# Attention beside a Fourier layer on one core: triangle selections one block after their softmax without a mark, and a store queued behind the next block's transposition

## Chip, cores and metric

One core of a Trainium2 chip runs the whole program. The metric is the device time of one execution in microseconds (us). Before the change it is 1834.63 us, the median of three runs (1828.07 to 1836.04).

## What is computed

Two independent layers on inputs of 2048 rows by 1024 columns, their outputs set side by side (2048 x 2048, fp32):

```
qkv    = (A_x @ A_wqkv), cut into 32 heads of width 32
scores = q @ k.T * 32**-0.5, kept where 0 <= i - j < 256, else -1e9
a      = concat_heads(softmax(scores) @ v) @ A_wo
b      = dft_seq_re @ (B_x @ dft_hid_re.T) - dft_seq_im @ (B_x @ dft_hid_im.T)
out    = concatenate([a, b], axis=-1)
```

The factors of the first layer are drawn eight times larger, so the softmax is sharp and the kernel works in pairs of fp16 numbers: every fp32 operand is split into a high and a low half (hi and lo), and a product is made of three matmuls (hi x hi, hi x lo, lo x hi).

## The kernel before

**The long products.** TensorE does almost nothing but matmuls of 128 x 128 weights against 512 columns, called products here. First come the projections of q, k and v (`product`, L341, matmuls on L347), then the Fourier layer: units of kind "x" (the hidden transform, again `product`) and units of kind "c" (the sequence transform, `seven`, L813, matmuls on L825, tiles p_a, p_b, p_c), and last the output projection (tiles po_a to po_c, also L825). Their operands are split by ScalarE (ACT) and VectorE (DVE), and ACT and DVE empty their accumulators (tiles y, L817 and L819).

**Attention in small blocks among them.** `attention` (L175) is a generator. Every eight product matmuls (four in `seven`) call `tick`, which lets it take its next step when it is due. There are 256 blocks: 8 groups of 4 heads, 4 chunks of 512 rows, 2 halves of the heads (2 heads each), 4 rows of 128 queries. Step b, with halves j = 0 and 1, does this:

- `s_step` (L197): the scores of one head by matmul (L214) into tile s, two buffers in PSUM. After the second head (j = 1) the softmax of the block: DVE masks the corner by a predicated copy (L222) and takes the maximum mx (L224); ACT makes the bias (L227), the exponentials (L234, one per head) and the high half hi (L237); DVE makes the low half lo (L238). Both go to tile hl, and SyncE (SP) issues a DMA that transposes hl into t (L240). Tile t has the packed weights of at most two key blocks: where a row of queries sees three, the first and the last are both triangles and share one square.
- `z_step` (L243): parts that packed square on GpSimd (POOL). A first selection writes one triangle to tile z (L252, four buffers), a second clears it from t in place (L254).
- `v_step` (L258): weights times values for a pair of blocks (e, e+1), e even, by matmul (L282) into tile pv (one PSUM bank, which the transposes of `scale_of` use too); the pair's second block comes first, and it needs that block's z and t. DVE divides by the row sums (L288 to L293) into tile o. It is issued LAG = 6 steps after the pair's first block.
- `o_step` (L298): every eight blocks, ACT and DVE split o into ohl; SP transposes it by DMA into ot (L305) and stores ot to DRAM as ots (L306). o, ohl and ot share three buffers. ots is read only in the output projection at the end (`o_load`, L782, its DMAs on L786).

**What sets the order.** The code is recorded in the order above. A list scheduler then gives each engine its own fixed order: of the instructions that its timeline holds ready, the one recorded first. Each engine runs its order strictly and waits on semaphores where an operand or a buffer is not ready. So an instruction that is recorded early but is ready late in that timeline goes behind later ones, and one wait holds everything behind it on that engine. SP's order holds all loads, transpositions and plain stores; POOL's holds the selections, small fills, and the adding stores of the Fourier layer's results (L909). `tc.issue_after(x)` fixes an instruction behind x on x's engine.

**The mark.** After the bias of every odd block, POOL copies one column of it to tile mark (L231). Before the change the first selection of a block is fixed behind the latest mark, and so are the adding stores. `z_step` is called in pairs: at odd b, after block b's softmax is recorded, for blocks b-3 and b-2.

Of the kernel before, what the change touches and what calls it, by code (L numbers as in the profile page):

```python
# [16 lines left out]
ALU = mybir.AluOpType  # L17
AX = mybir.AxisListType

P = 128  # L20
# [30 lines left out]
def fused_kernel(ctx: ExitStack, tc: tile.TileContext, xa, wqk, wv, wo, xb, wd, cs, out):  # L51
    nc = tc.nc
# [4 lines left out]
    ots = tc.dram_tile((NCH, P, NG, 2, CH), F16, name="ots")  # L57
# [24 lines left out]
                            fill=0.0, base=0, pattern=[[1, P]], channel_multiplier=-1)  # L82
# [43 lines left out]
    marks = []  # L126
# [48 lines left out]
    def attention():  # L175
# [2 lines left out]
                  for hp in range(2) for i in range(QB)]  # L178
        nblk = len(blocks)
        st, cur, q2s, k2s, vts = {}, {}, {}, {}, {}  # L180

        def do_load(g, sc):
            if (g, sc) in q2s:
                return
            for d, kind, parts, bufs in ((k2s, 1, (0, 0, 1), 3), (q2s, 0, (0, 1, 0), 2)):
                u = att.tile([96, HG, CH], F16, tag=f"qk{kind}", bufs=bufs, name=f"qk{kind}_{g}_{sc}")
                for j, part in enumerate(parts):
                    nc.sync.dma_start(u[32 * j:32 * j + 32],
                                      qs[kind, g, sc, part].rearrange("(h d) t -> d h t", d=DH))
                d[g, sc] = u  # L190

            vt = att.tile([P, QB, HG * VW], F16, tag="vt", bufs=3, name=f"vt_{g}_{sc}")
            nc.sync.dma_start(vt, vs[sc * QB:sc * QB + QB, :, g * HG * VW:(g + 1) * HG * VW]
                              .rearrange("t p c -> p t c"))
            vts[g, sc] = vt

        def s_step(b, j):  # L197
            g, sc, hp, i = blocks[b]
            qb = sc * QB + i
            nb = min(qb + 1, 3)  # L200
            if j == 0:
                if i == 0:
                    do_load(g, sc)
                st[b] = {"s": ps_s.tile([P, 2, 512], F32, tag="s", name=f"s_{b}")}
            if j == 1 and hp == 1 and i == 0 and b + QB < nblk and (g, sc + 1) in ready:
                do_load(*blocks[b + QB][:2])
            d = st[b]
            h = 2 * hp + j
            s = d["s"]
            k0 = qb + 1 - nb  # L210
            while k0 <= qb:
                k1 = min(qb + 1, (k0 // QB + 1) * QB)
                at = (k0 - (qb - 2)) * P
                nc.tensor.matmul(s[:, j, at:at + (k1 - k0) * P], q2s[g, sc][:, h, i * P:i * P + P],  # L214
                                 k2s[g, k0 // QB][:, h, k0 % QB * P:k0 % QB * P + (k1 - k0) * P],
                                 start=True, stop=True, skip_group_check=True)
                k0 = k1
            if j == 0:
                return
            w = min(nb, 2) * P  # L220
            sv = s[:, :, 3 * P - w:3 * P]
            nc.vector.copy_predicated(s[:, :, 2 * P:3 * P], upper2, s[:, :, :P] if nb == 3 else never2)  # L222
            mx = att.tile([P, 2], F32, tag="mn", bufs=6, name=f"mx_{b}")
            nc.vector.tensor_reduce(mx, sv, axis=AX.X, op=ALU.max, negate=True)  # L224
            bias = att.tile([P, 2], F32, tag="bias", bufs=6, name=f"bias_{b}")
            es = esc[g][:, sc:sc + 1]
            nc.scalar.activation(bias, mx, AF.Identity, bias=pshift, scale=es)  # L227
            if b % 2 == 1:

                mark = att.tile([P, 1], F32, tag="mark", bufs=2, name=f"mark_{b}")  # L230
                marks[:] = [nc.gpsimd.tensor_scalar(mark, bias[:, 0:1], 1.0, None, op0=ALU.mult)]  # L231

            for h in range(2):
                nc.scalar.activation(sv[:, h], sv[:, h], AF.Exp, bias=bias[:, h:h + 1], scale=es)  # L234
            hl = att.tile([P, 8 * P], F16, tag="hl", bufs=3, name=f"hl_{b}")
            hi, lo = (hl[:, a * w:a * w + 2 * w].rearrange("p (h k) -> p h k", h=2) for a in (0, 2))
            nc.scalar.activation(hi, sv, AF.Copy)  # L237
            behind[:] = [nc.vector.tensor_tensor(lo, sv, hi, op=ALU.subtract)]  # L238
            t = att.tile([P, 8, P], F16, tag="t", bufs=6, name=f"t_{b}")
            nc.sync.dma_start_transpose(t[:, :4 * min(nb, 2)], hl[:, :4 * w])  # L240
            d["t"] = t

        def z_step(b):  # L243

            g, sc, hp, i = blocks[b]
            if sc * QB + i < 2:
                return
            d = st[b]
            pk = d["t"].rearrange("p (a k) q -> p a k q", k=2)[:, :, 1]
            z = att.tile([P, 4, P], F16, tag="z", bufs=4, name=f"z_{b}")  # L250
            with tc.issue_after(marks[0].ins):
                nc.gpsimd.affine_select(out=z, in_=pk, compare_op=ALU.is_gt, fill=0.0, base=0,  # L252
                                        pattern=[[0, 4], [-1, P]], channel_multiplier=1)
            nc.gpsimd.affine_select(out=pk, in_=pk, compare_op=ALU.is_ge, fill=0.0, base=0,  # L254
                                    pattern=[[0, 4], [1, P]], channel_multiplier=-1)
            d["z"] = z
# [41 lines left out]
        def o_step(g, sc):  # L298

            o = cur.pop((g, sc)).rearrange("p i c -> p (i c)")  # L300
            ohl = att.tile([P, 2, CH], F16, tag="o", bufs=3, name=f"ohl_{g}_{sc}")
            nc.scalar.activation(ohl[:, 0], o, AF.Copy)
            nc.vector.tensor_tensor(ohl[:, 1], o, ohl[:, 0], op=ALU.subtract)
            ot = att.tile([P, 2 * QB, P], F16, tag="o", bufs=3, name=f"ot_{g}_{sc}")
            nc.sync.dma_start_transpose(ot, ohl.rearrange("p h c -> p (h c)"))  # L305
            nc.sync.dma_start(ots[sc, :, g].rearrange("c h t -> c (h t)"), ot.rearrange("p a q -> p (a q)"))  # L306

        for b in range(nblk + LAG):
            for j in range(2):
                yield blocks[b][:2] if b < nblk else None  # L310
                if b < nblk:
                    s_step(b, j)
                if j == 1 and b % 2 == 1 and 3 <= b < nblk + 3:
                    z_step(b - 3)
                    z_step(b - 2)
                if j == 0 and b % 2 == 0 and b >= LAG:
                    v_step(b - LAG)
                    g, sc, hp, i = blocks[b - LAG + 1]
                    if hp == 1 and i == QB - 1:
                        o_step(g, sc)  # L320

    acc = [0.0]
    agen, upcoming = [None], [None]
# [385 lines left out]
    with tc.tile_pool(name="pa", bufs=2) as pa:  # L709
        for n, (kd, g, c) in enumerate(order):  # L710
# [4 lines left out]
            if n == START:  # L715
                agen[0] = attention()
                upcoming[0] = next(agen[0])
# [3 lines left out]
            if kd == "v":  # L721
                t = c
# [127 lines left out]
    with tc.tile_pool(name="pb", bufs=1) as pb:  # L850
# [56 lines left out]
        def store(dst, src):  # L907
            with tc.issue_after(marks[0].ins):
                nc.gpsimd.dma_start(dst, src, accum_op=ALU.add)  # L909
# [6 lines left out]
        for n, (kind, p, c, i) in enumerate(units):  # L916
            if kind == "x":
# [13 lines left out]
                else:  # L931
                    a = pair.pop()
# [92 lines left out]
```

## Time and profile before

| what | us |
|---|---|
| median of three runs | 1834.63 |
| lowest and highest run | 1828.07, 1836.04 |
| span of the profiled execution, first to last instruction | 1822.3 |
| TensorE busy in it | 1756.3 |
| VectorE, ScalarE, GpSimd busy | 1325.8, 1093.0, 406.9 |

No run time is listed for the profiled execution by itself; its span is 12.3 us below the median of the runs, which is what lies around the span together with the difference between runs. TensorE busy time counts each matmul with its latency, so a busy TensorE may still lose time; idle time is certain loss. In the profile PE is TensorE, PEld its weight loads, and "idle before" is what an instruction's engine waited just ahead of it.

### The profile page before, as it was taken

The numbers are of one execution on the slowest core, as the hardware profiler recorded it, in microseconds if no ns is written. First come the engines' busy times: TensorE is split into PE (matmuls) and PEld (weight loads), VectorE is DVE, ScalarE is ACT, GpSimd is POOL, SyncE is SP. The second block draws the span as 40 slices with busy tenths as digits, with TensorE's granted clock in tenths as the row PEclk, the third lists the DMA queues.
The fourth block names the chain that finished last, engine by engine and source line by source line (L and its number), as shares of the span: only waits on it lengthen the run. The fifth ranks groups of instructions, "written<-read, shape, count | busy, mean of one in ns | idle before, by whom it ended". The sixth has DMA issues, their size and how long they took to land.

```text
span 1822.3 us, 30052 instructions
## 1 busy us (share of the span) xinstructions
PE 1756.3 (96%) x10876; PEld 857.3 (47%) x10876; DVE 1325.8 (73%) x2362; ACT 1093.0 (60%) x1867; POOL 406.9 (22%) x666
## 2 busy tenths in 40 slices
PE   7999999999999999999989899998989999999998
PEld 3444545555545544555444444544544554444443
DVE  7665887778766788886788686888876788577442
ACT  3333554556556777776777676777776678463322
POOL 0000222222212222322123233323333223200000
PEclk9999999999999999999999999999999999999999
DMA  5357898978767656899548989756998746855331
GB/s 231 115 176 209 211 249 216 237 176 215 183 144 166 128 123 156 183 197 214 111 100 173 197 182 199 162 127 128 188 176 191 151 93 128 226 109 98 110 93 70
DMA packets 440598, 297.96 MB, mean 164 GB/s; under 512 B 339072, under 2 KB 396416, under 8 KB 440448
## 3 DMA queue, kind: packets, MB, share of 16 engines
q1 hardware_dynamic: 433536, 270.87, 62.1%
q0 software_dynamic: 6912, 25.17, 8.4%
q8 instruction: 85, 1.39, 0.3%
q14 instruction: 65, 0.53, 0.1%
HBM read 146.93 MB, written 75.63 MB: 122 GB/s over the span
## 4 chain that ended last, share of the span: by engine, by line
PE 73%; DVE 9%; issue 7%; DMA 6%; ACT 4%; POOL 2%; SPq 0%; POOLq 0%; DVEq 0%; ACTq 0%
PE p L347 13%; PE p_a L825 10%; PE pv L347 9%; PE pk L347 9%; PE pq L347 8%; PE p_b L825 5%; PE po_a L825 5%; DMA t<-hl 3%; PE s L214 3%; PE pv L282 3%; PE p_c L825 3%; PE po_b L825 2%; PE po_c L825 1%; DVE raw_u L626 1%; DMA out_dram<-reg 1%
## 5 line engine op out<-in xcount | busy, mean ns | idle before, releaser
L347 PE MATMUL p<-reg,un 128*128 128x512 f16 x1536 | 345.1, 379 | 0.0
L234 ACT ACTIVATE s<-s,bias,escs 128x256 f32<-128x256 f32 (+1 forms) x512 | 267.4, 528 | 10.6
L227 ACT ACTIVATE bias<-mx,pshift,escs 128x2 f32<-128x2 f32 x256 | 97.5, 383 | 242.7 <-DVE mx L224 210.8
L231 POOL TENSOR_SCALAR mark<-bias 128x1 f32<-128x1 f32 x128 | 42.8, 334 | 846.0 <-ACT bias L227 831.5
L347 PEld LDWEIGHTS <-un 128*128 128x128 f16 x1536 | 146.5, 98 | 164.9
L238 DVE TENSOR_TENSOR hl<-s,hl 128x512 f16<-128x512 f32 (+1 forms) x256 | 169.7, 666 | 74.5 <-ACT hl L237 72.5
L825 PE MATMUL p_a<-reg,un_c 128*128 128x512 f16 x768 | 186.0, 384 | 6.4 <-ACT p_c L832 4.9
L347 PE MATMUL pq<-reg,wu_q 128*128 128x512 f16 x768 | 177.8, 386 | 6.9 <-ACT reg L113 4.3
L254 POOL TENSOR_SCALAR_AFFINE_SELECT t<-t 128x512 f16<-128x512 f16 x224 | 181.2, 881 | 0.1
L347 PE MATMUL pk<-reg,wu_k 128*128 128x512 f16 x768 | 175.1, 379 | 0.9 <-ACT wu_k L113 0.5
L347 PE MATMUL pv<-reg,reg 128*128 128x512 f16 x768 | 174.0, 379 | 0.0
L224 DVE TENSOR_REDUCE mx<-s 128x2 f32<-128x512 f32 (+1 forms) x256 | 169.5, 666 | 2.4
L252 POOL TENSOR_SCALAR_AFFINE_SELECT z<-t 128x512 f16<-128x512 f16 x224 | 155.4, 712 | 48.9 <-DMA t<-hl 48.3
L237 ACT ACTIVATE hl<-s 128x512 f16<-128x512 f32 (+1 forms) x256 | 148.3, 583 | 9.8 <-DMA t<-hl 5.0
L222 DVE COPY_PREDICATED s<-upper,s 128x256 f32<-128x256 uint32 x224 | 94.0, 422 | 60.1 <-PE s L214 55.5
L214 PE MATMUL s<-qk,qk 96*128 96x128 f16 (+2 forms) x704 | 128.7, 276 | 3.4 <-DVE hl L238 3.4
L282 PE MATMUL pv<-vt,t 128*128 128x65 f16 x1984 | 114.3, 186 | 11.6 <-POOL t L254 11.2
L347 PEld LDWEIGHTS <-wu_q 128*128 128x128 f16 x768 | 75.3, 99 | 96.0 <-issue 13.2
L825 PEld LDWEIGHTS <-un_a 128*128 128x128 f16 x768 | 74.8, 99 | 93.1 <-issue 8.5
L825 PEld LDWEIGHTS <-un_c 128*128 128x128 f16 x768 | 74.4, 99 | 92.6 <-issue 10.2
L825 PEld LDWEIGHTS <-un_b 128*128 128x128 f16 x768 | 73.4, 98 | 89.2 <-issue 5.3
L282 PEld LDWEIGHTS <-t 128*128 128x128 f16 x1984 | 97.8, 97 | 35.1 <-POOL t L254 14.9
(175 smaller groups left out, 2873.1 us busy)
## 6 DMA issues: line engine op xcount, KB each, us to landing
raw_u<-in_cs_dram SPq DMA_DIRECT2D x64, 512.0 KB, 4.8
qk<-qs SPq DMA_DIRECT2D x192, 128.0 KB, 3.2
out_dram<-y POOLq DMA_DIRECT2D x36, 512.0 KB, 7.5
raw_u<-in_xb_dram SPq DMA_DIRECT2D x32, 512.0 KB, 5.2
vs<-yv SPq DMA_DIRECT2D x32, 260.0 KB, 2.8
vt<-vs SPq DMA_DIRECT2D x32, 260.0 KB, 4.3
raw_x<-in_xa_dram SPq DMA_DIRECT2D x16, 512.0 KB, 10.2
qs<-yq SPq DMA_DIRECT2D x32, 256.0 KB, 2.2
```

Of the source, the lines that this page charges most:

```text
L214: nc.tensor.matmul(s[:, j, at:at + (k1 - k0) * P], q2s[g, sc][:, h, i * P:i * P + P], k2s[g, k0 // QB][:, h, k0 % QB * P:k0 % QB * P + (k1 ...
L222: nc.vector.copy_predicated(s[:, :, 2 * P:3 * P], upper2, s[:, :, :P] if nb == 3 else never2)
L224: nc.vector.tensor_reduce(mx, sv, axis=AX.X, op=ALU.max, negate=True)
L227: nc.scalar.activation(bias, mx, AF.Identity, bias=pshift, scale=es)
L234: nc.scalar.activation(sv[:, h], sv[:, h], AF.Exp, bias=bias[:, h:h + 1], scale=es)
L237: nc.scalar.activation(hi, sv, AF.Copy)
L238: behind[:] = [nc.vector.tensor_tensor(lo, sv, hi, op=ALU.subtract)]
L252: nc.gpsimd.affine_select(out=z, in_=pk, compare_op=ALU.is_gt, fill=0.0, base=0, pattern=[[0, 4], [-1, P]], channel_multiplier=1)
L254: nc.gpsimd.affine_select(out=pk, in_=pk, compare_op=ALU.is_ge, fill=0.0, base=0, pattern=[[0, 4], [1, P]], channel_multiplier=-1)
L282: nc.tensor.matmul(pvt[:, r, j, lo:], weights(part, j, kb), vts[g, k // QB][:, k % QB, at + lo:at + VW], start=(m == 0), stop=(m == len(se ...
L347: nc.tensor.matmul(ps, lhs(hl, d), rhs(hr, d), start=(m == 0), stop=(m == 3 * n - 1))
L825: nc.tensor.matmul(ps, lhs[pos](hl, k), rhs(pos)[:, hr, k], start=(m == 0 and pos < 2), stop=(m == 11), skip_group_check=True)
```

## The change

Three edits. The selections of a block are called one step after its softmax, block by block (`z_step(b - 1)` at every step), in place of two blocks at a time, two and three steps after. Their tie to the mark goes; the marks stay, for the adding stores. The store of ot is kept back in a list and recorded after the transposition of the next block whose softmax is recorded, fixed behind it on SP; after the last blocks it is issued at once.

```diff
+        held_back = []
...
-            nc.sync.dma_start_transpose(t[:, :4 * min(nb, 2)], hl[:, :4 * w])
+            moved = nc.sync.dma_start_transpose(t[:, :4 * min(nb, 2)], hl[:, :4 * w])
             d["t"] = t
+            for store in held_back:
+                with tc.issue_after(moved.ins):
+                    store()
+            held_back.clear()
...
-            with tc.issue_after(marks[0].ins):
-                nc.gpsimd.affine_select(out=z, in_=pk, compare_op=ALU.is_gt, fill=0.0, base=0,
-                                        pattern=[[0, 4], [-1, P]], channel_multiplier=1)
+            nc.gpsimd.affine_select(out=z, in_=pk, compare_op=ALU.is_gt, fill=0.0, base=0,
+                                    pattern=[[0, 4], [-1, P]], channel_multiplier=1)
...
-            nc.sync.dma_start(ots[sc, :, g].rearrange("c h t -> c (h t)"), ot.rearrange("p a q -> p (a q)"))
+            held_back.append(lambda: nc.sync.dma_start(ots[sc, :, g].rearrange("c h t -> c (h t)"),
+                                                       ot.rearrange("p a q -> p (a q)")))
...
-                if j == 1 and b % 2 == 1 and 3 <= b < nblk + 3:
-                    z_step(b - 3)
-                    z_step(b - 2)
+                if j == 1 and 1 <= b < nblk + 1:
+                    z_step(b - 1)
...
                         o_step(g, sc)
+                        if b >= nblk:
+                            held_back.pop()()
```

## The prediction

> **What bounds the kernel.** I read the page's busy shares first, then busy time by stretches, cut where TensorE's busy tenths change, then who waited for whom.
>
> ```profile
> PE 1756.3 (96%) x10876; PEld 857.3 (47%) x10876; DVE 1325.8 (73%) x2362; ACT 1093.0 (60%) x1867; POOL 406.9 (22%) x666
> ```
> ```profile
> 98.00:950.00 852.00, 848.04 (x5556) 423.72 (x5554) 644.75 (x1206) 526.15 (x935) 195.75 (x356) 1.00 0.75 178
> 950.00:1556.00 606.00, 568.99 (x3772) 281.92 (x3771) 472.88 (x877) 432.80 (x764) 199.61 (x286) 0.98 0.80 161
> ```
>
> The second block's columns are the stretch, its length, then busy time of PE, PEld, DVE, ACT and POOL, the granted clock, the DMA share and GB/s. TensorE is the bound. From 98 to 950 us it idles 4 us of 852, so nothing that helps attention can gain there. From 950 to 1556 it idles 37 us of 606, at a mean clock of 0.98: that is where the change can act for the better. After 1556 there is almost no attention left.
>
> What TensorE waits for in that stretch, and what lies behind it:
>
> ```profile
> PE pv L282 <- POOL t L254: 11.2, 11, 2.2
> PE pv L282 <- POOL z L252: 10.1, 3, 6.1
> POOL z L252 <- DMA t<-hl: 41.9, 21, 6.6
> SPq L306 <- DMA ot<-ohl: 16.7, 9, 4.3
> ```
>
> The figures are total us, times, longest. Waits of the value matmuls on the selections (21.3 us here) are the largest part of the 37. POOL in its turn waits 21 times for a transposition that has not landed. SP waits nine times with the store of ot for its transposition, and what stands behind it waits too. The worst case shows the links (SP first, then POOL, then PE):
>
> ```profile
> 948.65 1.24 SPq L305 DMA_TRANSPOSE ot<-ohl  x1
> 954.28 0.33 SPq L306 DMA_DIRECT2D ots<-ot  x1
> 954.71 2.69 SPq L240 DMA_TRANSPOSE t<-hl  x2
> ```
> ```profile
> 954.55 0.21 POOL L231 TENSOR_SCALAR mark<-bias 128x1 f32<-128x1 f32 x1 [8.03 <-ACT bias L227]
> 954.71 0.64 POOL L252 TENSOR_SCALAR_AFFINE_SELECT z<-t 128x512 f16<-128x512 f16 x1
> 958.14 0.71 POOL L252 TENSOR_SCALAR_AFFINE_SELECT z<-t 128x512 f16<-128x512 f16 x1 [2.80 <-DMA t<-hl]
> ```
> ```profile
> 958.90 0.23 PE L282 MATMUL pv<-vt,z 128*128 128x65 f16 x1 [6.05 <-POOL z L252]
> ```
>
> The transpositions stood behind the store, which stood behind ot's landing; both mark and landing were late, and the landing came last. So a mark alone is not what TensorE waits for here.
>
> **Clock.** Stretches cut at the clock's steps:
>
> ```profile
> 956.53:963.35 6.82, 3.96 (x31) 1.87 (x32) 4.57 (x8) 2.88 (x6) 2.34 (x3) 0.50 0.51 116
> 1031.50:1033.70 2.20, 0.24 (x3) 0.01 (x1) 2.20 (x3) 0.71 (x2) 2.14 (x2) 1.00 0.88 165
> 1035.03:1038.45 3.42, 3.42 (x10) 1.23 (x9) 1.89 (x5) 1.65 (x4) 0.21 (x1) 0.50 1.12 208
> 1272.00:1274.40 2.40, 0.17 (x3) 0.05 (x1) 2.40 (x4) 2.40 (x5) 2.35 (x2) 1.00 0.87 207
> 1362.71:1369.54 6.83, 6.35 (x36) 3.00 (x37) 2.85 (x7) 2.11 (x5) 2.24 (x5) 0.50 0.83 237
> 1550.45:1553.86 3.41, 3.41 (x29) 1.76 (x30) 2.32 (x5) 0.00 (x0) 3.34 (x4) 0.50 0.97 183
> ```
>
> Four stretches at half clock, 20.5 us together, follow or hold such waits: about 10.2 us of lost product time, 0.48 us for each of the 21.3 us waited.
>
> **The change part by part.** No instruction is added or removed but order; 448 selections and 32 stores move.
>
> *Mark and early calls.* A pair's selections, which stood behind the bias of a block two later, may now start when their packing lands. On paper that removes at most the 21.3 us and the 10.2 us of clock: 31.5 us. One buffer rule takes part of the advance: with four buffers z, the selection of an even block e must wait for the value matmuls of pair e-4. Those stand ahead of the scores of e+1 in the new order, or within 1 us of them, well before e's packing can land, so I price this wait at nothing; without that cover it would hold marks, fills and adding stores behind it on POOL. These stores also come behind selections that wait for a landing; they write tiles y, of which there are four, and POOL is busy only 199.6 of 606 us, so nothing again, at worst some us.
>
> *Store kept back.* SP no longer stands still for the 16.7 us; at most the nine cases with it gain. ots is read at the very end, and the buffer of ot is wanted a chunk (eight blocks) later, which hides the delay; if it did not, DVE's write of o would wait.
>
> *What the scheduler makes of it.* This is the term that decides. I counted in the fixed order of both kernels how many 512-column products stand on TensorE between the last score matmul of a pair's second block and the pair's first value matmul. That count is the time that softmax, transposition and selection have before TensorE stops. For the first 49 pairs (to about 670 us) the orders of TensorE are the same: 96.9 products on the mean. For the other 79 pairs it falls from 80.7 to 55.2; for the last 30 from 79.5 to 49.7, mostly exactly 48. The value matmuls stay where they were among the products; the scores stand later. A product costs 0.216 us:
>
> ```profile
> 109.06 20.72 PE pk L347 x96
> ```
>
> So 5.5 us of slack is gone on the mean, 6.4 us at the end, and 17.4 us of products become 11.9 (10.7 at the end). Scores and an earlier value group in between add about 1.7 us at most (estimate: the timeline's 0.49 us for two score matmuls, twice, and some 0.7 us for narrow matmuls), so 13.6 us on the mean, 12.4 at the end.
>
> Against it, the chain from scores to selected triangles, by rows:
>
> ```profile
> L234 ACT ACTIVATE s<-s,bias,escs 128x256 f32<-128x256 f32 x214 | 111.0, 528 | 3.4
> L254 POOL TENSOR_SCALAR_AFFINE_SELECT t<-t 128x512 f16<-128x512 f16 x98 | 91.5, 1069 | 0.1
> L238 DVE TENSOR_TENSOR hl<-s,hl 128x512 f16<-128x512 f32 x109 | 72.4, 668 | 38.2 <-ACT hl L237 38.0
> L224 DVE TENSOR_REDUCE mx<-s 128x2 f32<-128x512 f32 x107 | 70.5, 665 | 0.5
> L252 POOL TENSOR_SCALAR_AFFINE_SELECT z<-t 128x512 f16<-128x512 f16 x98 | 70.4, 732 | 41.9 <-DMA t<-hl 41.9
> L237 ACT ACTIVATE hl<-s 128x512 f16<-128x512 f32 x109 | 63.1, 584 | 6.4 <-DMA t<-hl 5.0
> L227 ACT ACTIVATE bias<-mx,pshift,escs 128x2 f32<-128x2 f32 x107 | 40.4, 382 | 69.2 <-DVE mx L224 66.3 <-DVE sc_u L107 1.3 <-DVE rs L288 1.1
> L222 DVE COPY_PREDICATED s<-upper,s 128x256 f32<-128x256 uint32 x95 | 39.5, 421 | 21.8 <-PE s L214 20.2 <-PE pv L282 1.0
> ```
> ```profile
> DMA to landing us min/median/max: 2.4/3.8/15.0
> ```
>
> Bare, with nothing in the way: 0.42 + 0.67 + 0.38 + 2 x 0.53 + 0.58 + 0.67 = 3.8 us to the low half, 3.8 us median landing, 0.73 + 1.07 us of selection: 9.4 us. That fits. But DVE is busy 78% and ACT 71% of this stretch, and the landing reaches 15 us. A pair as it ran (PE scores, SP, POOL, PE values):
>
> ```profile
> 1271.62 0.49 PE L214 MATMUL s<-qk,qk 96*128 96x384 f16 x2
> 1294.59 0.19 PE L282 MATMUL pv<-vt,z 128*128 128x65 f16 x1
> ```
> ```profile
> 1277.89 5.64 SPq L240 DMA_TRANSPOSE t<-hl  x2
> ```
> ```profile
> 1291.17 0.94 POOL L252 TENSOR_SCALAR_AFFINE_SELECT z<-t 128x512 f16<-128x512 f16 x1 [0.25 <-DMA t<-hl]
> ```
>
> Its values came 22.5 us after its scores, with 84 products between (block 206). The new order leaves 50 there: 34 x 0.216 = 7.3 us less, 15.2 us. Its packing landed 19 us after the scores. TensorE would have stood about 5 us.
>
> *The sum.* In the stretch POOL waited for landings in 21 cases; 98 selections z are 49 pairs. Such a landing comes after the mark of a block one pair later. A pair passes every 606 / 49 = 12.4 us and its mark needs 0.42 + 0.67 + 0.38 us, so it is at least 13.9 us after the scores, plus a mean wait of 2.0, plus 1.8 of selection: 17.7 us, against 12.9 us (between the two means above): 4.8 us late, 21 times: 101 us. But the next pair's scores mostly stand just ahead of the waiting value matmul, so one pair's wait is slack for the next one: I take half, 50 us (bounds: nothing, if every chain is bare; 101, if none is relieved). At 0.48 us of clock each, 24 us more. Off go 21.3, 10.2, and half of SP's 16.7. Before 950 us the slack is larger, about 15 us; I add 2 us. Sum: 50 + 24 - 21.3 - 10.2 - 8.3 + 2 = +36 us on a span of 1822.3. Added to the median, 1834.63 + 36 = **1871 us**.
>
> *A rule weighed.* The clock term rests on the 1031.50 row (2.2 us almost idle, half clock soon after) against the 1272.00 row (2.4 us, no such stretch shown). The Trainium skill, TensorE: Matmul & The Clock Gate, Part 1, has the clock halve after an idle window of about 3.4 us that runs freely; the stretches of 3.41 and 6.83 us agree with that window, the 1031.50 row shows that less idling can do. By that page alone waits of 2 to 3 us would mostly cost no clock; that is rival 2.
>
> **Rivals.**
>
> 1. *Faster: the chain is close to bare.* Place: the landing of the second block's packing. If it comes within about 11 us of the scores (13 less 1.8), the value matmuls never wait, and the whole 21.3 + 10.2 us goes: 1803 us; with some waits left, up to 1825. For it: 9.4 us bare, SP free of its 16.7, scores later and so less crowded by earlier work. Against: 21 landings of 49 are beyond 13.9 us. Chance 0.20.
> 2. *Waits without clock.* As forecast, but short waits cost no half clock: 36 - 24 = +12, 1847 us. Chance 0.10.
> 3. *No relief.* The chain's own DVE and ACT steps stand behind work that waits for the same stopped TensorE, so each wait comes in full: 101 + 48 - 21.3 - 10.2 - 8.3 + 2 = +111, 1946 us. For it: in the new order the low half of block 207 stands on DVE behind a product's add that needs TensorE 6.5 us on; 6.5 + 0.67 + 3.8 + 1.8 = 12.8, already over 12.3. Chance 0.07.
> 4. *Like for like.* Old waits go, as many come: 1835 us. The change then does not do what it says in effect, though it moves all it names. Chance 0.08.
>
> **How the numbers follow.** Forecast, chance 0.55: 1871, itself 1847 to 1908 (new waits of 34 to 75 us for the 50, each with its clock). To hold 8 in 10, the range leaves out rival 3 (0.07) and the faster half of rival 1 (0.10): 1812 to 1925. A measurement here tells about 0.5% from no change, 9 us. Faster by more: rival 1, 0.20. Within: rival 4 and a fifth of rival 2, 0.10. Slower by more: the rest, 0.70.
>
> **What the new profile would show.** Right: TensorE's waits on z and t after 680 us come to 40 to 60 us in some 20 to 40 cases, spread over pairs and not only beside ot's stores; POOL's idle time before z is put down to the landing, more than 41.9 us; half-clock stretches in greater number; SP's wait with the store near nothing; 98 to 650 us unchanged. Wrong: few such waits, landings within 11 us of the scores (rival 1); or new waits of the products themselves on DVE or ACT, which the reordering may bring and for which I have no row.

## The result, and the profile after

| | before | after |
|---|---|---|
| median (lowest to highest), us | 1832.38 (1828.07 to 1836.04) | 1899.41 (1897.04 to 1906.29) |
| ratio to before, 95% interval | | 1.038 (1.035 to 1.0411) |
| profiled execution: time, span, us | span 1822.3 | 1906.29, 1904.6 |

The change makes the kernel 3.8% slower: 67 us between the medians, 82.3 us between the two profiled spans. In the execution after only 1.7 us lies around the span, so the "12.3 us" of the text above was nearly all difference between runs: with 1.7 us around its span, the profiled execution of before took some 1824 us, under the lowest time listed, while that of after is the longest of its four. What follows accounts for the 82.3 us.

The busy shares of the page, then its stretches with the same columns as before:

```profile
PE 1783.0 (94%) x10876; PEld 862.9 (45%) x10876; DVE 1329.4 (70%) x2362; ACT 1093.5 (57%) x1867; POOL 435.5 (23%) x666
```
```profile
98.00:650.00 552.00, 551.30 (x3567) 274.98 (x3566) 402.11 (x753) 301.01 (x536) 128.64 (x239) 1.00 0.79 191
650.00:950.00 300.00, 291.61 (x1937) 145.17 (x1934) 242.99 (x443) 220.50 (x391) 86.31 (x114) 1.00 0.66 154
950.00:1556.00 606.00, 525.58 (x3331) 254.90 (x3330) 409.60 (x766) 378.79 (x669) 178.88 (x248) 0.94 0.72 146
```

The kernel before had, in the first two of these stretches:

```profile
98.00:650.00 552.00, 551.12 (x3567) 274.98 (x3565) 401.19 (x753) 300.80 (x536) 118.11 (x237) 1.00 0.78 191
650.00:950.00 300.00, 296.92 (x1991) 148.74 (x1989) 243.56 (x454) 225.35 (x400) 77.64 (x119) 1.00 0.69 155
```

The same instructions run. From 98 to 650 us TensorE does not differ. By 950 us it is 54 matmuls behind. From 950 to 1556 it idles 80 us where it idled 37, at a mean clock of 0.94 where it was 0.98, and gets through 441 matmuls fewer (3331 against 3772); all these run after 1556 us. Over the whole span, idle time of TensorE rises from 66.0 to 121.6 us (+55.6), and its busy time by 26.7 us with the same matmuls: the slower clock.

What TensorE waits for, by the waits (total us, times, longest):

```profile
PE pv L286 <- POOL z L256: 48.6, 20, 6.7
PE pv L286 <- POOL t L258: 13.2, 21, 1.5
PE p_a L831 <- DVE y L825: 7.7, 9, 2.1
PE p_a L831 <- ACT y L823: 7.7, 3, 4.4
PE s L215 <- DVE hl L239: 6.6, 3, 3.4
```

Waits of the value matmuls on the two selections are 61.8 us; over the whole trace of before they were 22.3 (+39.5):

```profile
PE pv L282 <- POOL t L254: 11.2, 11, 2.2
PE pv L282 <- POOL z L252: 11.1, 4, 6.1
```

The long products' waits on ACT and DVE (p_a, p_b, p_c, all rows) went from 15.9 to 28.0 us (+12.1), the scores' wait for their buffer from 3.4 to 6.6.

One pair shows how; it is the pair of block 206, which the prediction followed before. Scores of block 207, and its softmax, selection and values, from the timeline (start, length, engine, line, what it is, idle before):

```profile
1330.80 0.49 PE L215 MATMUL s<-qk,qk 96*128 96x384 f16 x2
...
1337.85 2.75 PE L831 MATMUL p_a<-reg,un_b 128*128 128x512 f16 x12
1340.56 2.75 PE L831 MATMUL p_a<-reg,un_a 128*128 128x512 f16 x12
1343.15 0.82 PE L215 MATMUL s<-qk,qk 96*128 96x128 f16 x6
1346.70 0.20 PE L286 MATMUL pv<-vt,z 128*128 128x65 f16 x1 [2.73 <-POOL z L256]
1346.74 0.20 PE L286 MATMUL pv<-vt,t 128*128 128x65 f16 x1
1348.28 0.20 PE L286 MATMUL pv<-vt,t 128*128 128x65 f16 x1 [1.35 <-POOL t L258]
```
```profile
1333.49 0.38 ACT L228 ACTIVATE bias<-mx,pshift,escs 128x2 f32<-128x2 f32 x1
1333.77 1.14 ACT L113 ACTIVATE un_a<-raw_u,sc_u 128x1024 f16<-128x1024 f32 x1
1334.81 0.71 ACT L113 ACTIVATE reg<-raw_u,sc_u 128x512 f16<-128x512 f32 x1
1335.42 1.05 ACT L619 ACTIVATE junk<-raw_u 128x1024 uint8<-128x1024 f32 x1
1336.37 0.19 ACT L619 ACTIVATION_READ_ACCUMULATOR junk<-raw_u 128x1 f32 x1
1336.46 1.09 ACT L235 ACTIVATE s<-s,bias,escs 128x256 f32<-128x256 f32 x2
```
```profile
1340.43 0.68 DVE L239 TENSOR_TENSOR hl<-s,hl 128x512 f16<-128x512 f32 x1
```
```profile
1341.13 3.65 SPq L241 DMA_TRANSPOSE t<-hl  x2
```
```profile
1346.00 0.64 POOL L256 TENSOR_SCALAR_AFFINE_SELECT z<-t 128x512 f16<-128x512 f16 x1 [8.29 <-DMA t<-hl]
```

Counted from the end of the scores, as in the prediction, the values come after 15.4 us; before it was 22.5. The packing lands after 14.7 us; before it was 19. So the chain did get shorter, but less than the room did, and TensorE stands 2.73 + 1.35 us. Of the chain, 2.6 us pass between the bias and the exponentials, in which ACT works on another operand (L113, L619); 2.2 more between the end of the high half (0.60 us on ACT, from 1337.58) and the low half on DVE; and 4.9 us from the issue to the landing. Waits like this come about every 26 us from 1300 to 1510 us.

### The profile page after: what moved, and what is told of

Same layout as the page of the kernel before. It is cut to its first block, busy times and chain, and to the rows that moved or that the text cites. A ratio compares the mean times of both kernels' runs of the same rounds, so it can differ in the third digit from the quotient of the medians.

```text
span 1904.6 us, 30082 instructions
## 1 busy us (share of the span) xinstructions
PE 1783.0 (94%) x10876; PEld 862.9 (45%) x10876; DVE 1329.4 (70%) x2362; ACT 1093.5 (57%) x1867; POOL 435.5 (23%) x666
## 4 chain that ended last, share of the span: by engine, by line
PE 67%; DMA 11%; DVE 10%; ACT 5%; issue 3%; POOL 3%; SPq 0%; POOLq 0%; DVEq 0%; ACTq 0%
PE p L353 10%; PE p_a L831 9%; PE pv L353 9%; PE pk L353 9%; PE pq L353 8%; DMA t<-hl 8%; PE p_b L831 5%; PE po_a L831 4%; PE pv L286 3%; PE p_c L831 3%; PE s L215 3%; PE po_b L831 2%; DMA out_dram<-y 2%; POOL z L256 1%; DMA out_dram<-reg 1%
## 5 line engine op out<-in xcount | busy, mean ns | idle before, releaser
L256 POOL TENSOR_SCALAR_AFFINE_SELECT z<-t 128x512 f16<-128x512 f16 x224 | 171.4, 765 | 878.9 <-DMA t<-hl 774.5
L353 PE MATMUL p<-reg,un 128*128 128x512 f16 x1536 | 349.9, 381 | 1.4 <-ACT reg L930 1.4
L286 PE MATMUL pv<-vt,z 128*128 128x65 f16 (+1 forms) x896 | 98.3, 188 | 48.9 <-POOL z L256 48.6
L831 PEld LDWEIGHTS <-un_a 128*128 128x128 f16 x768 | 77.4, 102 | 101.5 <-issue 21.3
L831 PEld LDWEIGHTS <-un_b 128*128 128x128 f16 x768 | 73.6, 98 | 95.1 <-issue 12.3
## 6 DMA issues: line engine op xcount, KB each, us to landing
raw_x<-in_xa_dram SPq DMA_DIRECT2D x16, 512.0 KB, 10.2
```

Of the source, the lines that this page charges most:

```text
L286: nc.tensor.matmul(pvt[:, r, j, lo:], weights(part, j, kb), vts[g, k // QB][:, k % QB, at + lo:at + VW], start=(m == 0), stop=(m == len(se ...
L353: nc.tensor.matmul(ps, lhs(hl, d), rhs(hr, d), start=(m == 0), stop=(m == 3 * n - 1))
L831: nc.tensor.matmul(ps, lhs[pos](hl, k), rhs(pos)[:, hr, k], start=(m == 0 and pos < 2), stop=(m == 11), skip_group_check=True)
```

## The experiments

Each kernel ran beside the kernel before on the same chip; that had a median of 1830.39 us beside the first four, 1831.94 beside the next four, 1825.46 beside the last three. So the ratios are to be compared, not the medians. "Products" is the count on which the prediction rests: 512-column products on TensorE between the last score matmul of a pair's second block and its first value matmul, mean of the 79 pairs from block 98 on. "Selections" is TensorE's wait on z and t, "half clock" the time at a granted clock of 0.5 from 98 us to the last matmul, both from the profiled execution.

| kernel | products | selections, us | half clock, us | median, us | ratio (interval) |
|---|---|---|---|---|---|
| before | 80.7 | 22.3 | 27.3 | | 1 |
| after | 55.2 | 61.8 | 78.5 | 1899.41 | 1.038 (1.035 to 1.0411) |
| held store alone | 80.7 | 23.6 | 27.3 | 1825.07 | 0.9977 (0.9954 to 1.0) |
| mark's tie out, early calls | 61.1 | 60.6 | 78.5 | 1893.87 | 1.0345 (1.0297 to 1.0393) |
| after, five buffers z | 55.2 | 59.2 | 85.3 | 1901.49 | 1.0394 (1.0336 to 1.0453) |
| after, products behind scores (2) | 78.1 | 31.2 | 51.2 | 1837.27 | 1.0037 (1.001 to 1.0064) |
| early calls, mark kept | 59.1 | 43.8 | 61.4 | 1874.61 | 1.0229 (1.0198 to 1.026) |
| after, products behind scores (4) | 65.3 | 53.3 | 64.9 | 1881.4 | 1.0292 (1.0238 to 1.0346) |
| after, products behind scores (1) | 88.1 | 19.7 | 51.2 | 1823.98 | 0.9961 (0.9935 to 0.9987) |
| held store, behind scores (1) | 87.3 | 31.3 | 54.6 | 1824.94 | 0.9968 (0.9942 to 0.9995) |
| held store, (1) from block 151 | 83.5 | 31.7 | 41.0 | 1821.37 | 0.9969 (0.9948 to 0.9991) |
| after, (1) from block 151 | 76.6 | 17.5 | 41.0 | 1825.76 | 1.0003 (0.9978 to 1.0028) |
| held store, (1) blocks 151 to 196 | 81.4 | 24.1 | 34.1 | 1819.82 | 0.997 (0.9946 to 0.9995) |

The theory was the prediction's: the change takes products, that is time, from between a pair's scores and its values. Rivals: the selections off the mark wait for their own buffers; the missing tie to the mark itself; the store.

**The store alone.** The held-back store of the change on the kernel before, nothing else. The orders of TensorE, DVE, ACT and POOL are those of before; only SP's differs.

> Only the held-back store; selections and mark as before. The fixed orders of TensorE, VectorE, ScalarE and GpSimd are those of before, and only 83 places of SP's order differ. Theory 1 (the scores stand too close ahead of the value matmuls, 55 products in place of 81, so the chain from scores to selections does not fit): here 81 products stand, so no loss; SP's 16.7 us of waits with the store go, and part of TensorE's 21 us of waits on selections with them: 0 to 12 us faster than before, 1820 to 1833 us. Rival 3 (the later store, or what it crowds, is the cause): slower than before by 20 us or more.

Measured: 1825.07 us. SP's wait with the store, 37.1 us in 26 cases over the whole trace of before, is nearly gone (SP's waits of this kernel):

```profile
SPq L311 <- DMA ot<-ohl: 5.8, 5, 1.9
```

TensorE's waits stay (23.6 us against 22.3). The store does no harm; its gain is 0.2%, at the edge of the interval, though 31 us of waiting on SP went.

**The mark out and early calls, the store as before.**

```diff
-            with tc.issue_after(marks[0].ins):
-                nc.gpsimd.affine_select(out=z, ...
+            nc.gpsimd.affine_select(out=z, ...
...
-                if j == 1 and b % 2 == 1 and 3 <= b < nblk + 3:
-                    z_step(b - 3)
-                    z_step(b - 2)
+                if j == 1 and 1 <= b < nblk + 1:
+                    z_step(b - 1)
```

> The mark's tie is gone and the selections are called one block behind, the store stands as before. 61 products stand between scores and value matmuls after pair 98 (81 before, 55 in the changed kernel). Theory 1: most of the loss is here, scaled by products lost 20/25.5 of 67 us, so about +50 us, 1870 to 1895 us. Rival 3: near before, 1832 us.

Measured: 1893.87 us, nearly the whole loss. TensorE's waits of this kernel:

```profile
PE pv L281 <- POOL z L251: 49.2, 20, 7.0
PE pv L281 <- POOL t L253: 11.4, 20, 1.3
```

The loss is in these two edits. The store, added to them, takes the count on from 61.1 to 55.2, but the two ratios can't be told apart. Of the two edits, the call by single blocks does nothing once the tie is gone: with the tie out and the calls left in pairs, two and three blocks late, every engine gets the same order, instruction by instruction (seen in the fixed orders; that kernel did not run). So without the tie a selection gets the same place, recorded early or late; only the tie had held it back.

**Five buffers z** (`bufs=4` to `bufs=5` in the changed kernel; TensorE's order stays).

> The changed kernel with five buffers z in place of four; orders of all engines but GpSimd's are the same, and GpSimd's differs in 22 places. Theory 1: the 81 us that GpSimd waits for TensorE before a selection lie beside the landing of the transposition, so the time stays within 10 us of the changed kernel, 1889 to 1905 us. Rival 2 (the selection of an even block waits for a buffer that the value matmuls two pairs back give free, and that wait is what makes TensorE late): most of the loss goes, 1835 to 1860 us.

Measured: 1901.49 us. The waits of the selections for free buffers fall, in POOL's waits of this kernel,

```profile
POOL z L256 <- DMA t<-hl: 807.4, 163, 16.5
...
POOL z L256 <- PE s L215: 25.5, 6, 6.4
```

from 55.0 us in 11 cases behind scores in the changed kernel, and those behind values from 25.9 to 9.6 (those behind p_a rise, from 11.5 to 26.2). POOL now waits the longer for landings (807.4 against 774.5), TensorE waits 59.2 us for selections where it waited 61.8, and nothing is gained. That rival falls: the buffer is not what comes last.

**Products fixed behind scores.** In `seven`, the first matmul of each accumulation is fixed behind a block's last score matmul, on TensorE. The list `scored` holds that matmul of every block recorded so far, and the block is the n-th from its end (n = 2 here). The selections, the missing mark, the early calls and the store are those of the changed kernel.

```diff
-                    nc.tensor.matmul(ps, lhs[pos](hl, k), ...
+                    with tc.issue_after(scored[-2].ins) if m == 0 and len(scored) < 256 else nullcontext():
+                        nc.tensor.matmul(ps, lhs[pos](hl, k), ...
```

> The changed kernel, with the first matmul of each accumulation in the sequence transform and output projection fixed behind the score matmuls of the block two recorded before: TensorE may not run its products further ahead of the scores. 78 products stand between scores and value matmuls after pair 98. Selections, mark and store are as in the changed kernel. Theory 1: TensorE's waits on selections fall from 62 us to below 20 us and the time to 1820 to 1850 us, unless scores now wait for their own buffer. Rival 2: waits and time stay as in the changed kernel, 1890 us or more.

Measured: 1837.27 us. 62 of the 67 us come back with every one of the change's edits in place (TensorE's waits of this kernel):

```profile
PE pv L288 <- POOL z L258: 21.7, 11, 6.3
PE s L216 <- DVE hl L241: 11.3, 6, 4.2
PE pv L288 <- POOL t L260: 9.5, 16, 1.6
```

Selections are at 31.2 us, above the 20 us that I had set; scores that stand earlier wait for their own buffer (11.3 us). So the cause lies in the order, not in the selections.

One rival is left: fixing the products moves the orders of ACT and DVE as well, and a less crowded chain would also shorten the waits. The traces, matched instruction by instruction with the fixed orders, speak against it. They give, for the 70 pairs from block 98 on that have selections, the chain (from the end of the second block's scores to the end of its first selection) and the room (from the same point to where TensorE reaches the first value matmul). The mean chain is 14.5 us in the changed kernel and 14.4 here; the mean room is 15.4 us there and 19.5 here, and the chain outlasts it in 21 pairs there, in 12 here. In the kernel before they are 17.2 and 20.6 us, with 4 such pairs: the change did shorten the chain, but it took more from the room.

**Early calls with the mark kept.**

> Only the early call by single blocks is made; the tie to the mark stays and the store stands as before. In the fixed order 59.1 products stand between a pair's scores and its values (all but the first 49 pairs), against 80.7 before and 55.2 after. Theory (lost slack): the time follows that count, whatever moved it: 1870 to 1895 us, and TensorE waits 45 to 65 us for the selections. Rival (the missing mark itself does the harm, because selections taken off it stand ahead of work that TensorE needs): the mark is still here, so 1825 to 1840 us with waits under 30 us.

Measured: 1874.61 us. The mark and its tie are still there and the kernel is 2.3% slower, so most of the loss doesn't need their absence. Waits for selections are just under the 45 to 65 us expected. But the count is not the whole of it. With 59.1 products this kernel waits 43.8 us for selections; the one without the tie, at 61.1, waits 60.6 us and takes 19 us longer, though about as many pairs are late in both (21 and 20). What else differs between these two is not settled.

**65 products** (n = 4 in the changed kernel).

> The changed kernel, with the first matmul of each long accumulation fixed behind the scores of three blocks back, not of one block back as in the run with 78.1 products: 65.3 products stand between a pair's scores and its values. Theory (lost slack), in proportion: the changed kernel has 1899 us at 55.2 and the run before had 1837 at 78.1, that is 2.7 us per product, so 1872 us (1858 to 1885), with 40 to 50 us of waits for selections. Rival (a threshold: what harms is only the pairs of 48 products): under 1850 us, since few pairs of 48 are left. Rival (fixing anything behind scores cures it): 1837 us again.

Measured: 1881.4 us (three runs at 1881 to 1882, one at 1900.51), 9 above the proportional 1872 and inside its range; waits for selections 53.3 us, a little over the 40 to 50 expected. Fixing products behind scores cures nothing as such, and the rival of a threshold, under 1850 us, falls too: the wait grows as the room shrinks.

**88 products** (n = 1 in the changed kernel).

> The changed kernel, with the first matmul of each long accumulation fixed behind the last scores recorded: 88.1 products between a pair's scores and its values, more than before (80.7). Theory (lost slack): waits for selections under 20 us and 1820 to 1832 us. Rival (scores that stand earlier wait for their own buffer, which the softmax of two blocks before must free): TensorE waits for the predicated copy and the maximum, 10 us and more ahead of the scores, and the time is 1840 to 1860 us.

Measured: 1823.98 us, 0.4% below the kernel before, with 19.7 us of waits for selections. The rival's mechanism is there as well, 14.5 us of scores waiting for their buffer (TensorE's waits of this kernel), but it doesn't outweigh the gain:

```profile
PE pv L288 <- POOL z L258: 16.0, 4, 4.7
PE s L216 <- DVE hl L241: 14.5, 8, 3.9
```

**More room for the kernel before** (held store, mark and paired calls kept, n = 1).

> The kernel before with the held-back store, the tie to the mark and the paired calls kept, and the first matmul of each long accumulation fixed behind the last scores recorded: 87.3 products against 80.7. Theory (lost slack): some of the 23.6 us of waits that the held-back store alone leaves go: 1810 to 1822 us. Rival (scores wait for their buffer): 1830 to 1850 us.

Measured: 1824.94 us, the same as with the store alone, and a miss: waits for selections did not fall (31.3 us). Its stretches, against the kernel with the store alone, show why (first the store alone, then this kernel):

```profile
650.00:950.00 300.00, 297.11 (x1991) 148.89 (x1989) 243.23 (x454) 225.11 (x399) 77.31 (x119) 1.00 0.67 156
950.00:1200.00 250.00, 231.47 (x1523) 114.44 (x1522) 193.64 (x355) 176.85 (x307) 86.73 (x118) 0.98 0.90 179
1200.00:1556.00 356.00, 335.11 (x2240) 166.56 (x2239) 276.57 (x521) 254.55 (x455) 113.34 (x166) 0.98 0.74 145
```
```profile
650.00:950.00 300.00, 284.68 (x1913) 143.10 (x1912) 243.08 (x448) 220.47 (x391) 81.55 (x122) 0.97 0.65 156
950.00:1200.00 250.00, 246.47 (x1659) 123.84 (x1658) 203.20 (x372) 187.27 (x326) 79.74 (x121) 1.00 0.87 182
1200.00:1556.00 356.00, 330.35 (x2171) 164.92 (x2169) 272.28 (x511) 251.56 (x444) 109.44 (x163) 0.95 0.74 146
```

TensorE gains 15 us of busy time from 950 to 1200 us, and gives back 12 ahead of that stretch and 5 behind it.

**Room only where TensorE waits.** Three kernels fix products behind scores (n = 1) from block 151 on only (condition `151 <= len(scored) < 256`; the third up to 196).

> The kernel before with the held-back store, and long accumulations fixed behind the last scores only from block 151 on (after about 950 us); up to there the order is that of the held-back store alone. Theory (slack where TensorE waits, and nowhere else): the run with the order fixed everywhere had 15.3 us idle between 650 and 950 us against 2.9 with the store alone, and 29 us between 950 and 1556 against 39; taking the better of both gives 1823.2 - 10 = 1813 us (1806 to 1818), 0.985 to 0.992 of the kernel before. Rival (the idle time moves on with the order and comes back elsewhere): 1822 to 1828 us, as the store alone.

> The changed kernel (no mark, early calls, held-back store), with long accumulations fixed behind the last scores from block 151 on; before that the order is the changed kernel's, with 59.8 products between scores and values in blocks 98 to 146 (after it 84). Theory (lost slack, where TensorE is the bound): 8 us idle between 650 and 950, as in the changed kernel, and after that as with 88 products everywhere (27.7 us idle up to 1556): 1815 us (1810 to 1822). Rival (the missing mark harms by itself): 1830 us and more.

> As the kernel with the slack added from block 151 on, but only for blocks 151 to 196 (about 950 to 1190 us): 87 products there, 78.6 after it. Theory (slack where TensorE waits): after 1200 us the fixed order gained nothing (73.4 us idle-free loss of busy time in 1200 to 1556 with it, 71.4 in the kernel before), so 1813 us again (1806 to 1820). Rival (the gain is spread over all late blocks): 1818 to 1826 us.

Measured: 1821.37, 1825.76 and 1819.82 us, with ratios of 0.9969, 1.0003 and 0.997. The hoped-for 10 us did not come: the two with the mark's tie stand where the store alone stood, whose interval covers them. The second lies outside both of its expected ranges; the third lies in both of its, which overlap there, so it decides nothing between them. The idle time moved, as the rival of the first had it (the third kernel's stretches; the 15 us gained are now 8, and 7.5 are lost ahead of them; the store alone has the rows shown above):

```profile
650.00:950.00 300.00, 289.61 (x1943) 145.41 (x1942) 242.70 (x455) 223.94 (x399) 79.77 (x124) 0.98 0.69 158
950.00:1200.00 250.00, 239.28 (x1585) 118.81 (x1584) 195.89 (x356) 179.99 (x312) 80.60 (x118) 0.99 0.91 178
```

The second kernel has no tie to the mark, and with 76.6 products it equals the kernel before: its rival (the missing mark harms by itself, 1830 us and more) falls at this room. Where the products stand counts beside their mean: with 78.1 products (n = 2) the changed kernel stayed 0.4% slower than the kernel before, and it has 75 of them after block 146, where TensorE waits most; this kernel has 84 there. From 81 products on, more room buys nothing that can be told from the store's own 0.2 to 0.3%. No version beat the kernel before by more than half a per cent.

## Why the prediction was right, and where it was off

The sign and the mechanism held; 1899 lies in the range, 28 us above the forecast. By its steps:

- **What bounds.** Right. All the loss lies after 650 us, and most of it from 950 on.
- **What the scheduler makes of it.** Right, and it is the cause: giving the products back (55.2, then 65.3, 78.1, 88.1) takes the time to 1881, 1837 and 1824 us with the change's edits in place, and with 78.1 the room grew while the chain stayed.
- **New waits, 50 us.** Too small. The forecast left 22.3 - 21.3 + 50 + 2 = 53 us of waits on selections; there were 61.8 (+9). That it came so near is in part luck. The chain did outlast the room in 21 pairs, the forecast's number, but only 12 of these had a selection that waited for its landing before. These 21 were 2.3 us late on the mean up to the first selection, not 4.8: the half made up for that, and whether relief between pairs is the reason is not shown. The 101 us of no relief was far off.
- **Waits of the products themselves.** Named as a danger without a row, and priced at nothing: they and the scores' waits grew by 12.1 + 3.2 us, and waits straight on a landing by 1.9. This is the largest single miss, +17 us. That a standing TensorE delays what feeds ACT and DVE, and then waits for them, would explain it. The record agrees: these two kinds of waits come to 26 to 35 us in the five kernels that wait 43 us or more for selections, to 11 to 24 in the others. No run tests it.
- **Clock.** The rate held, the amount didn't. Half clock after 98 us grew from 27.3 to 78.5 us, 25.6 us of lost product time where 24 - 10.2 = 13.8 was forecast (+12). Per us of all new idle time (25.6 / 55.6) that is 0.46, forecast 0.48. Rival 2 (no clock loss) is out.
- **The store, -8.3 us.** Wrong as a term. SP's waits went as foreseen, but TensorE's did not follow: 22.3 us before, 23.6 with the store alone. The worst case that I had shown was read rightly, but the half that I took for the sum was not in the trace. By its ratio the store alone is worth 4 us (0 to 8), and beside the other two edits nothing shows (1893.87 us without it, 1899.41 with it).
- **The sum.** 36 + 9 + 17 + 12 + 8 = 82 us, against 82.3 us of span. Adding it to the median rather than to the span hid part of this: the medians differ by 67 us.
- **The mark.** It was called not what TensorE waits for. That stands; but its tie, with calls two and three blocks late, also set where the scheduler put scores and values, and removing the tie or moving the calls early was each enough to lose the room (61.1 and 59.1 products). The price for the buffers z, nothing, was right (five buffers gain nothing), but not its reason: POOL did wait behind score and value matmuls, 80.9 us in 23 cases, and with a fifth buffer it waited for landings instead.
- **The signs to look for.** 40 to 60 us in 20 to 40 cases: 61.8 in 41, just above both, spread over pairs. SP's wait with the store fell from 37.1 to 9.5 us. POOL's idle time on landings, "more than 41.9", was a poor sign: it is 774.5 us over the whole trace, but POOL waited 831.5 us for the bias with the mark before and waits 128.3 now, so most of it has only changed its place.

**The rule weighed.** The runs decide it for the 1031.50 row: short waits do cost clock. Two pairs of stretches of the changed kernel, the first after the two waits of the pair shown above:

```profile
1345.28:1348.69 3.41, 0.64 (x17) 0.53 (x18) 2.45 (x4) 2.49 (x6) 2.62 (x3) 1.00 0.86 215
1348.69:1352.10 3.41, 3.41 (x22) 1.47 (x19) 1.99 (x5) 0.49 (x2) 0.94 (x3) 0.50 0.54 161
```
```profile
1423.79:1427.20 3.41, 1.44 (x11) 0.71 (x9) 2.90 (x5) 2.46 (x3) 0.79 (x2) 1.00 1.15 254
1427.20:1430.61 3.41, 2.94 (x29) 1.63 (x28) 3.29 (x7) 2.45 (x5) 2.88 (x4) 0.50 0.91 263
```

A window in which TensorE was busy 0.64 us, or as much as 1.44 us of 3.41, is followed by one at half clock. The Trainium skill, TensorE: Matmul & The Clock Gate, Part 1, has the gate watch a free-running window of 3.41 us; the trace agrees, since the half-clock stretches lie on one grid of 3.413 us. The page asks for an idle window; here windows with 0.64 and 1.44 us of work were enough, and the measurement decides.

## What to carry to other kernels

Before an ordering tie is taken off in a kernel whose order a scheduler makes, count in both fixed orders how much of the bounding engine's work stands between a producer and its consumer: here 25 products fewer per pair cost 67 us, though with the tie in place TensorE had waited only 22.3 us for the selections. If a tie must go, what it did for the order can be kept by fixing the long work behind the producer, which brought 62 us back; past some 81 products, more room only moved the idle time elsewhere. A wait that goes on an engine off the path, as SP's 31 us did, is worth only what the bound engine's own waits show.

## What the runs showed of the hardware

The granted clock goes by fixed windows of 3.413 us and by how busy TensorE is in each. Over the thirteen profiles, from 98 to 1640 us and among windows that ran at full clock: of 97 windows with under 1.4 us of TensorE busy all 97 were followed by half clock, of 45 with 1.4 to 1.8 us 22 were, and of 5516 with more than 1.8 us none. Each window at half clock costs 1.7 us of product time, so a wait of a little over 2 us costs either nothing or most of its own length again, by where it falls on the grid: in the changed kernel the wait of 2.27 us that ends at 1105.26 us lies in one window and was followed by half clock, that of 2.29 us that ends at 1482.14 us left its window 1.44 us of work and was followed by none.
